# Forgetting attention and a feed-forward layer on one core: one more token group by seven half products, score tiles paired across batches, the last product but one in halves, and a new order

## The chip, the core and the metric

The kernel runs on one core of a Trainium2 chip. The engines of the core (TensorE or PE, VectorE or DVE, ScalarE or ACT, GpSimd or POOL, SyncE or SP) each run their own list of instructions in order and wait for one another by semaphores; PEld is TensorE's loading of weights. The metric is the device time of one execution in microseconds (us); lower is better. 359.41 us is the median of 3 runs of the kernel before (358.56 to 359.49).

## The reference

The inputs are q, k and v of 8 batches, 8 heads, 576 tokens and 64 dimensions, a forget gate f for each token of each head, and three weights with a vector of gains. Cut to what matters:

```python
scores = q @ k.T / sqrt(64)
cum    = cumsum(log(clip(f, 1e-4, 1)))             # along the tokens
scores = where(causal, scores + cum_i - cum_j, -1e9)
o      = softmax(scores) @ v                       # 8 batches, 8 heads, 576 x 64
x      = o as 4608 tokens x 512
xn     = x / sqrt(mean(x * x) + 1e-6) * rms_g
out    = (silu(xn @ w_gate) * (xn @ w_val)) @ w_out     # 512 -> 1536 -> 512
```

## The kernel before

Attention works by batch. Keys lie on the partitions and queries on the columns, in blocks of 128 tokens; the last block has 64. A *score tile* is the product of one block of keys with one block of queries for all 8 heads (128 x 1024, in PSUM), and for the last 64 queries one tile holds two blocks of keys. So a batch has 10 tiles in its four whole query blocks and 3 for its last one. Heads have only 64 dimensions, so TensorE holds the scores' matmuls (L525) in another tiling, two side by side of 64 rows each. One *score block* is the matmuls of up to two tiles in a row. ScalarE takes the exponential (L544), GpSimd masks the tiles on the diagonal (L552), TensorE multiplies with the scaled values (L573; the gates' decay is folded into these values, and an added column gives the denominators), and VectorE divides (L592, L596). ScalarE and GpSimd make the norm (L621, L626, L627, L635). q and k are turned by DMA (L435), for the first two batches on TensorE (L450, L456), and so are the normed tokens (L643 in the first batch).

The feed-forward layer works on 9 groups of 512 tokens: group g below 8 is the first 512 tokens of batch g, and group 8 gathers the last 64 tokens of all batches. Groups 0 to 6 go the plain way: for each of 12 blocks of 128 of the 1536 middle dimensions there is one product with w_gate and one with w_val, each of 4 matmuls with 512 columns (L830, *gates* in this text), a tanh on ScalarE (L842) and two VectorE operations (L844, L837). Groups 7 and 8 use `seven()` instead: the product is split into 2 x 2 halves and computed from 7 half products in place of 8, each 4 matmuls with 256 columns (L765). That needs differences of token halves (L754), sums of weight halves once (L732), copies on ScalarE (L782, L784, L787), additions on VectorE (L790, L792), silu on ScalarE (L800, L810), and the product of the two branches on VectorE (L806) or on GpSimd (L816). The table for silu is loaded behind the last exponential (L733), since exp and silu don't share one.

The output product of every group is by seven too (`project`): TensorE L905, sums of its left side L880 to L889, copies L912, additions L915, and stores L933 and L935 on the queues of SP and ScalarE. In the last group one product is computed in two halves, so that its first half is added and stored while the second is computed.

What sets the order: the program records *units* (a few instructions of one engine with what they need and which buffer slots they hold). A table ORDER gives each unit its place in one common list, and a table SLOTS gives each buffer its slot; every engine then runs its instructions in the order of that list. Nothing is decided while the kernel runs. All loads of q, k, w_gate (wg), w_val (wv) and of the first batches' v are issued by GpSimd (L332, L344, L355, L365), between its masks.

In the rows, `ff` and `late` are PSUM buffers of TensorE's products (`late` are the four that served the scores until those were over), `sc` the score tiles, `PT` the exponentials (later 32-bit buffers of group 7 and 8), `sm` the sums of the output product, `hT` the middle layer, `ores` the output.

Of the kernel before, what the change touches and what calls it, by code (L numbers as in the profile page):

```python
# [29 lines left out]
SEVEN = {7, 8}  # L30
# [9 lines left out]
    "iomEmFkzkAl5l6kgkhl0l1kQkRlKlLjRjSlylzkqkr0s0B0v0J0S0M0P0W0I0N0O0T0X0Y18141a1c1i1m1q1s1w1D11191b1d1r"  # L40
    "1B1J1F1P1Z1U241v1Q2q2M3u213g2T3q3w333r3z3E3G353F3L3R3Q3X4e4a4g4q4u4D4J5f4z4M4U535m5g5q4G4H58592R5x5V"
    "5L5W5Z624n4o4X4Y5U646f6U6r6F6J6d6e5G5H7c6v6k6l5n5o7p7a7g7l7j5S5T65666x7u7y807H7P7W878p7r7s6s6t7C8g8n"
    "8x8G8V8I8P7F7G7Y7Z7w919c969m9y9D6D6E85868w888u8v8l8maw9I9P9W9M8K8L9N9ObC9Va7ai9ZalauaCba9S9TasatbpbG"
    "bMbTc2c5cbciaTaUadae9dcjcCcpcwcAdcbNbOaAaBaDbfaIaJbrbsdkcOcUdecXc0c1cFcGd6d1d8dFdgdudBdPetcncodvdwel"
    "e0e5ebekepeweEcecfdDdEcqePfbeSfdfifmeiejeCeDdWfUereseXeYgmftfBfJfSfgfhfYfZgtg3g9gggugHgSgMgRgogpfQfR"
    "h2h0hdh5hthHhwhDhkhlgegfhshZiiiViMiOiThahbiaibijhmhShThJhKiuj7jljrjqjyjzi4i5kNjQjXkwk3kekBkkkoklkmjD"
    "jEiKkVl2lalflwlBlIjTjUiZj0lglYm1mpmbmlmqlulvl8l9lkjxlNlOk6k7n8mRmXn4n3mymzmfmgnwn7nnnsntnNnTnQnUlDlE"
    "lllmo0o2o5obojoFoxoEn1n2m8m9mLoLpwoSp2pkpo1517161h1g1n1t1x1I1L20232i2m2n2r3I3N3M4147494c4h4l544r4V5D"
    "5Q616b686g757t7I7L7U818q8y8D8J8H8R8Q8W959b9e9h9Q9Xa5aaafavaZb7bibnc4cacccgcDcWcMcVdndxdydIdJdOe4e7ec"
    "egeFeKeNeQeReWf1f4fXg8gcghgjgngYh7h3hehvhFhEi7iciqiyiGjbjkjKjWkZl4lblelnlqlQm2lVlZmcmjmsmwn5nenhnrnz"  # L50
    "nCnLnRnXoeo6oaoiomoQoUoVoXpHpT1j1u1A1E1G1C1H1O1T1Y2e2l2p2t2x2v2y2D2G2L8rbwcuf5f6464E4K5c5t5B575u5C5R"
    "6i6p6w6A6G6z6I6OdmfWhiktku8O90949o9r9s9f9i9j929l9p9v9z9A9B9G9Hjvldm7pqpraNbFbLbZcJcKcscxcycPd0d3d7da"
    "dbdddidjfEhLiHkXkYdZenexeGeLeMfufGfHeZf8fcfofrfsflfzfAh1jeooqlqmhChUhYipiviwimiIiJixj2j5jdjmjnjajfjg"
    "jAlsmioGoHlrlHlPmxn9nalTlWlXmdmCmIndninjmQmVmWnmpuq6q9qao7oholp0p6p7oqouovoPp4pbpspypzpepipjqkqpqFqL"
    "qM1K2u2c2o2A2k2z2s2w2F2E2X2J2N342O322W3138392Y373e4p3l3i3y1V2625272f222d282b2j363k3h3j3p3O403U454b3Z"
    "6a5s52675E5A6n3t3S3B3P3Y2K3a2S3d3m3f483o3s4f3n3x3v3A3H424i76704v7q6N7e5X6c63696j5K6C606o6W6V7d74797i"
    "7J8t838d8A6m6K6H6R716h6u6q6y6B7h827m7z8c6Z7k7b7f7o8z8M8F8N987x7X7K7V848b8k8j8o8s7n7D7v7E7ObYcmc3c6ct"
    "ahb6ayaFbcbkbAbqbubJa6aEajaqaMaVbob3bebx9YaragakazbbcdbtbXclbvbKbBbPbUbQcrchcvcBc9czckcEcIaHbdaSb0bj"
    "axaOaGaPaYfkfLfxfDfVdQfwdXeafIeueIeBeHeOdGeddLdTemfFfTfMg0g4e6eoeheqevdKdVdUdYe1eVf3f2fjfnfffpfqfvfy"
    "eyf7eJf0fehhhAhrhBhIfCg5fKfPgigkgwgsgvgEgDhcgIgNhjiUjuj1j6jCgqgTgPgUgZh6hGhnhxhNgOhqgXh4hugdgLglgrgQ"  # L60
    "hQi3hXi6i9iNjGjjjFjIhMhWhRhVi2ihj3iBiPjii8iridikizkpkGkxkMl7kakCkykDkIkOm6kWltmrjVlck0k4lhmNmUmTmYn0"
    "jLjZk9kdkfmvmGmHmKmPmJmZmOmSn6lJlSlRlUm5m0mhmamemmmkmBmAmDmMlilFlolClMp9phpgplppnJo9nMnSodofonokopos"
    "ozoYoKoRp5pcpxpnpvpDpmpCpBpEpGoWp3oZp1pdoTptp8pfpAoroJoCoIoMnAnGnEnFnOnVo3o1o4o8ocowotoyoDjYogq2q5no"
    "nIpaqOqopLpOqnqqpQpUpVq1qzpXq0qeqtqKqjqQqdqfqbqyqrqCqJqSqWqZqVr5qDqGqTrarlrZqXr3qxqPqEqNqYqUrbr2rkrn"
    "rhrBr0r4qHqRrcrfrjrirurCryrIr8rsrFrLrMrRrvrGr9rgrzrDrorrrArVrQs4s0sgrmrprKrXrwrErOs2sbsesaskrtrPslso"
    "snsqshsxrqrxrWrUrHrJrSs1rNrYs3s6s7sis8svs5sfs9scspstswsmsEsHsBsVrTssszt3sJsMt7tDsrsusjsDsAsysKsPt8te"
    "sZtksCsIsdsFsTsNsQsLt0t6sStbsOsWtEtMt4twtntrsYt1sRsUtdt5tit2tptstotRt9tctqtytmtttxtCtztLtGtVtgtIu6uf"
    "tHtJtBtN3T4L4m4w4F4Z4Q5r4d4C4I4R7M7N4W5b5a5p5l5F8S8T5P5Ybybz4N5M8h8i8E8Z939k9g9q9w9UbHbI9n9x979C8U9F"
    "iWiX9J9Ra2a39Ea4bVbWcLcZcQd5cHcNcTdtg6g7cYd2d9dhd4dliQiRdCdHezeAdfdqf9faigiLitjcilisiAiSk1k2iYj4jhjp"
    "jojwkbkcjHjMjOjPjBjJqAqBjNkjk8kUk5knkvkHmnmokikskLkPl3ljnfnglplAmtmulxlGm3m4nbnunlnyncnqnvnBoNoOnpnx"  # L70
    "nDnHnknKoAoBnPnWnYnZpFpZqgqhpIpWpKpPpJpNpSq3q7q8pMpRq4qcpYqsqvqwqIr1r6r7qiqurdretathtjtusGsXtftltXtY"
    "tvtAtKtPtFtQtTtUu3uauduetOtSu0u1tZu5u2uotWu4uiuuuyuzuwuxu7u9u8ucubuhumunujukuvuFuIuJuGuHugulurusupuq"
    "utuAuDuEuBuC")
SLOTS = (
    "751b7a63635242211938006514304071702032672611556343322a53745b716946107b411165046361283342572233750170"
    "0a332b5330447841512610233962121b43705800557a606704213b46125269710710236153322a65015453732879107b4233"
    "614622043701427063180553291b406753613a26323322117030156104312200101106701300145111032106711011001542"
    "0107301411062100141051054321010107337106210451501711125602301030110560142030171010506016310112116104"
    "2721075101044106310476310520102701410101410761034060125107141010600265113014347017501124310601047101"
    "0351106702710213510761004450153017207106100053241230322211203053242032210101205204321003250240301350"  # L80
    "3324310313333003042321242100533423213430110125234132003331231102103220331301123162514033620133073520"
    "2152530072000633350711217010601120070304153612111000011112310201132002010301002000101310123101110032"
    "0113113300030021101011000013010210121132000010100103311230132001110120102103201101012112001220100100"
    "3001220101011011131001013011221102113210030011310210121011000321110112310011030011310000132000211011"
    "1022012100131023000311021102010111310120001010132002311301013012000121110000110101003111273604415751"
    "0064236357211106007124230037561153541106247213030100164145037112102430232017414210001232312173021020"
    "3303411200212030401233152252100206104015420120240002231242112014133200174232107211773642720120003124"
    "3471656523470")
# [960 lines left out]
```

## Time and profile before

| | us |
|---|---|
| median of 3 runs | 359.41 |
| the profiled execution | 359.02 |
| its span (first to last instruction) | 357.2 |
| TensorE busy | 340.5 |
| VectorE, ScalarE, GpSimd busy | 277.1, 252.8, 194.6 |

The profiled execution is a run like the others; 1.8 us of its time lie outside the span. The granted clock of TensorE is 0.999 of full speed over the span. Busy times of the engines overlap, so they don't add up to the span; that of TensorE is 95% of it.

### The profile page before, as it was taken

To read this page: it belongs to the slowest core of one execution; us is meant where nothing else is said; L and a number is where in the kernel's file an instruction comes from. 1 tells how busy PE (TensorE), PEld (TensorE's weight loads), DVE (VectorE), ACT (ScalarE), POOL (GpSimd) and SP (SyncE) were. 2 spreads that over 40 slices of the span, in tenths; PEclk is the share of its full clock that TensorE was granted. 3 is DMA by queue.
4 is the path that set the end of the run, shared out by engine and by line. 5 is a ranking of instruction groups with operands and counts; after the bars stand their busy time and mean duration, and the time that the engine had idled before them with its cause. 6 is when DMAs were issued, how large, how long until landed. Compare 5 with 4: busy or idle time off the path is not lost.

```text
span 357.2 us, 10310 instructions
## 1 busy us (share of the span) xinstructions
PE 340.5 (95%) x4202; PEld 250.6 (70%) x4202; DVE 277.1 (78%) x507; ACT 252.8 (71%) x417; POOL 194.6 (54%) x241
## 2 busy tenths in 40 slices
...
GB/s 126 218 202 225 198 144 89 142 137 181 160 140 165 165 221 111 154 131 139 142 154 144 152 131 151 135 149 146 61 29 83 54 2 140 61 2 0 2 106 131
DMA packets 161510, 44.86 MB, mean 126 GB/s; under 512 B 147060, under 2 KB 160888, under 8 KB 161464
## 3 DMA queue, kind: packets, MB, share of 16 engines
...
q8 instruction: 33, 0.54, 0.6%
q10 hardware_dynamic: 592, 0.52, 0.4%
...
## 4 chain that ended last, share of the span: by engine, by line
PE 80%; DVE 6%; DMA 4%; POOL 3%; issue 3%; ACT 2%; SPq 0%; DVEq 0%; POOLq 0%; ACTq 0%
PE ff L830 37%; PE ff L905 16%; PE sc L525 7%; PE ff L573 6%; PE ff L765 4%; PE late L765 4%; PE late L905 3%; DMA qk<-in_q_dram 2%; POOL qk L332 2%; DMA QT<-qk 1%; PE ff L456 1%; ACT PT L544 1%; DVE KT L754 1%; DVE ga L844 1%; DVE hT L837 1%
## 5 line engine op out<-in xcount | busy, mean ns | idle before, releaser
L544 ACT ACTIVATE PT<-sc 128x1024 bf16<-128x1024 f32 x96 | 95.7, 1024 | 20.3 <-PE sc L525 20.1
L830 PE MATMUL ff<-xT,wv 128*128 128x512 bf16 (+2 forms) x528 | 85.0, 302 | 0.3 <-DVE x L596 0.2
L830 PE MATMUL ff<-xT,wg 128*128 128x512 bf16 (+2 forms) x528 | 84.4, 301 | 0.8 <-DVE ores L915 0.3
L842 ACT ACTIVATE th<-ff 128x512 f32<-128x512 f32 x84 | 49.4, 599 | 30.9 <-PE ff L830 26.1
L844 DVE SCALAR_TENSOR_TENSOR ga<-th,ff 128x512 f32<-128x512 f32 x84 | 57.1, 683 | 17.6 <-ACT th L842 16.0
L837 DVE SCALAR_TENSOR_TENSOR hT<-ga,ff 128x512 bf16<-128x512 f32 x84 | 57.0, 684 | 16.1 <-PE ff L830 14.6
L552 POOL TENSOR_SCALAR_AFFINE_SELECT PT<-PT 128x1024 bf16<-128x1024 bf16 x32 | 36.4, 1138 | 49.2 <-ACT PT L544 48.1
L830 PEld LDWEIGHTS <-wg 128*128 128x128 bf16 x528 | 42.2, 98 | 24.9 <-issue 1.2
L830 PEld LDWEIGHTS <-wv 128*128 128x128 bf16 x528 | 41.5, 98 | 24.3 <-issue 0.7
L905 PEld LDWEIGHTS <-hT 128*128 128x128 bf16 x432 | 41.5, 98 | 6.5
L573 PEld LDWEIGHTS <-PT 128*128 128x128 bf16 (+1 forms) x896 | 32.7, 103 | 10.8 <-issue 1.9
L573 PE MATMUL ff<-Vs,PT 128*128 128x65 bf16 (+1 forms) x896 | 37.7, 196 | 0.4 <-POOL PT L552 0.4
L525 PE MATMUL sc<-QT,KT 64*128 64x128 bf16 (+1 forms) x960 | 34.5, 214 | 2.4 <-ACT KT L468 0.9
L915 DVE TENSOR_TENSOR ores<-ores,ff 128x512 f32<-128x512 f32 (+1 forms) x39 | 26.2, 671 | 13.0 <-PE ff L905 11.2
L596 DVE TENSOR_TENSOR x<-ff,rden 128x256 f32<-128x256 f32 (+1 forms) x80 | 33.9, 424 | 3.0 <-ACT xn L635 0.3
L525 PEld LDWEIGHTS <-KT 64*128 64x128 bf16 x960 | 24.9, 97 | 16.0 <-issue 12.7
L485 POOL TENSOR_TENSOR Vs<-v,decT 128x512 bf16<-128x512 f32 (+1 forms) x30 | 33.2, 1114 | 5.0 <-DMA v<-in_v_dram 4.9
L905 PE MATMUL ff<-wo,hT 128*128 128x256 bf16 x288 | 35.4, 273 | 0.0
L905 PEld LDWEIGHTS <-sm 128*128 128x128 bf16 x324 | 30.7, 98 | 5.2 <-DVE sm L886 0.9
L626 POOL TENSOR_SCALAR ms<-sq 128x2 f32<-128x2 f32 (+2 forms) x26 | 6.7, 260 | 50.5 <-ACT junk L621 48.8
L332 POOL DMA_DIRECT2D qk<-in_q_dram x36 | 31.2, 873 | 1.1 <-POOLq L1033 0.8
L332 POOL DMA_DIRECT2D qk<-in_k_dram x36 | 31.5, 880 | 0.4 <-issue 0.3
...
## 6 DMA issues: line engine op xcount, KB each, us to landing
...
qk<-in_q_dram POOLq DMA_DIRECT2D x28, 128.0 KB, 5.2
qk<-in_k_dram POOLq DMA_DIRECT2D x28, 128.0 KB, 5.5
...
wg<-in_moe_w_gate_dram POOLq DMA_DIRECT2D x3, 512.0 KB, 10.0
wv<-in_moe_w_val_dram POOLq DMA_DIRECT2D x3, 512.0 KB, 11.2
...
```

Of the source, the lines that this page charges most:

```text
L332: nc.gpsimd.dma_start(out=T_qk[h.slot][0:n, :].rearrange("p (h d) -> p h d", d=D), in_=src[b, :, p0:p0 + n, :].rearrange("h p d -> p h d"))
L485: eng.tensor_tensor(T_Vs[hv.slot][0:n, j, :, 0:D], T_v32[h.slot][0:n, :, :], bcast(dj, D), ALU.mult)
L525: nc.tensor.matmul(t[:, par, c:c + n], lhsT=kt[r, p, kj * 128:(kj + 1) * 128], rhs=qt[r, p, qi * 128:qi * 128 + n], start=not x, stop=True ...
L544: nc.scalar.activation(T_of_p[hp.slot][:, 0:2 * half].rearrange("p (a c) -> p a c", a=2)[:, :, 0:cols], T_sc[h.slot][:, :, 0:cols], ACT.Ex ...
L552: nc.gpsimd.affine_select(out=d, in_=d, pattern=[[0, 8], [1, n]], compare_op=ALU.is_ge, fill=0.0, base=0, channel_multiplier=-1)
L573: nc.tensor.matmul(T_ff[hpo.slot][r0:r0 + n, p * 65:p * 65 + 65], lhsT=T_of_p[h.slot][:, c:c + n], rhs=vs[:, kj, 2 * p + par, :], start=(k ...
L596: nc.vector.tensor_tensor(d, po[r0:r0 + n, :, 0:D], bcast(r[r0:r0 + n, :], D), ALU.mult)
L830: nc.tensor.matmul(T_ff[h.slot][:, c:c + n], lhsT=w[:, dc, fc * 128:(fc + 1) * 128], rhs=xT[:, dc, t0:t0 + n], start=(dc == 0), stop=(dc = ...
L837: nc.vector.scalar_tensor_tensor(hT, in0=three[0], scalar=0.5, in1=three[1], op0=ALU.mult, op1=ALU.mult)
L842: th = act(0.6, key - 0.1, lambda: nc.scalar.activation(T_th[ht.slot], T_ff[hg.slot], ACT.Tanh, scale=0.5), [ug], take=[ht])
L844: a = dve(0.69, key - 0.1, lambda: nc.vector.scalar_tensor_tensor(T_ga[ha.slot], in0=T_th[ht.slot], scalar=1.0, in1=T_ff[hg.slot], op0=ALU ...
L905: nc.tensor.matmul(t[:, s * HD:(s + 1) * HD], lhsT=a()[:, fc, s * 128:(s + 1) * 128], rhs=w[:, fc, :], start=(not more and s == ss[0] and ...
```

## The change

1. Group 6 is computed by seven half products too. The buffers for the differences of tokens were one for each of the two groups; now there are two slots which the three groups take in turn.
2. Each batch has 13 score tiles, an odd number. Before, the last tile of a batch was a block by itself. Now it makes a block with the first tile of the next batch, and 53 blocks take the place of 57.
3. In the last group a second output product (with `w22`, the half A of the output) is computed in two halves, each added and stored by itself; the buffers hold for the added stores.
4. ORDER and SLOTS are other tables.

```diff
-SEVEN = {7, 8}
+ACROSS = True
+SEVEN = {6, 7, 8}
...
 ORDER = (
-    "0302000104050h0j0k0A0w0l0o0g0i0C0p0z0a0b0F0Z1006070c0d08090e0f0m0n0t0u0x0y0q0r0D0E0K0L0Q0R1k1l0U0V12"
+    "03020001050604070H0v0t0s0y0i0j0m0n0u0c0d0z1C0D0g0h0e0f0a0b0k0l08090A0B0L0M0o0p0P0Q13141G1H26271f1g2m"
...
-                 sc=2, ff=4, hw=8, sw=8)
+                 sc=2, ff=4, hw=8, sw=8, xs=2)
...
-            if len(todo) == 2 or (b == 0 and kjs[-1] == qi) or kjs[-1] == LAST:
+            if len(todo) == 2 or (b == 0 and kjs[-1] == qi and qi < LAST) or kjs[-1] == LAST and (not ACROSS or b + 1 == B):
                 score_block(todo, qkey(b, qi, i))
                 todo = []
...
-        hs = spare[g - G]
+        hs = Hold("xs", 4 + 3 * 2 * 4)
...
-            return t[hs.slot].rearrange("p c t -> p (c t)")[:, 1536 + (i % 2) * 512:2048 + (i % 2) * 512].rearrange(
+            return t[spare[hs.slot].slot].rearrange("p c t -> p (c t)")[:, 1536 + (i % 2) * 512:2048 + (i % 2) * 512].rearrange(
...
-                       ready + ([X[need]] if need else []) + [Lsum["g", 1], Lsum["v", 1]], take=[hs], give=[hx])
+                       ready + ([X[need]] if need else []) + [Lsum["g", 1], Lsum["v", 1]], take=[hs], give=[hx, hs])
...
-            return pe(0.435, key, emit, deps, take=list(take), give=list(give) + [hx])
+            return pe(0.435, key, emit, deps, take=list(take), give=list(give) + [hx] + ([hs] if k in X else []))
...
-        o = [Hold("ores", 1 if g < B else 2 + 2 * (halved and i == 1)) for i in range(4)]
+        o = [Hold("ores", 1 if g < B else 2 + 2 * (halved and i < 2)) for i in range(4)]
...
-        m3 = product(lambda: T_sm[h4.slot], w22, f4, [m5, v4, u4], give=[h4], more=True)
-        store(A, 0, 1, plus(f4, A, A, [m3, v3], give=[f4]))
+        if not halved:
+            m3 = product(lambda: T_sm[h4.slot], w22, f4, [m5, v4, u4], give=[h4], more=True)
+            store(A, 0, 1, plus(f4, A, A, [m3, v3], give=[f4]))
         if halved:
-            f5.n = 2
+            f4.n = f5.n = 2
+            for s in range(2):
+                m3 = product(lambda: T_sm[h4.slot], w22, f4, [m5, v4, u4], give=[h4] if s else [], more=True, ss=(s,))
+                store(A, 0, 1, plus(f4, A, A, [m3, v3], c=slice(s * HD, (s + 1) * HD), give=[f4]), s)
```

Line numbers behind the diff's first lines are one higher in the changed kernel (L365 becomes L366, L552 becomes L553, and so on).

How the order moves is shown at three places. The first is GpSimd's queue while the kernel starts, before the change: loads of v, wg (w_gate) and wv (w_val) between the first masks (`AFFINE_SELECT`).

```order
L355 DMA v_69<-in_v_dram 128x8x64
L365 DMA wg<-in_moe_w_gate_dram 128x4x512 x2
L552 AFFINE_SELECT PT_82<-PT_82 128x1024
L365 DMA wv<-in_moe_w_val_dram 128x4x512
L552 AFFINE_SELECT PT_81<-PT_81 128x1024
L344 DMA wt<-in_k_dram 128x8x128
L365 DMA wv<-in_moe_w_val_dram 128x4x512
L365 DMA wg<-in_moe_w_gate_dram 128x4x512
```

The same queue after the change, from its third mask on (ms and rs are the norm's two small steps).

```order
L553 AFFINE_SELECT PT_77<-PT_77 128x1024
L356 DMA v_71<-in_v_dram 128x8x64
L627 TENSOR_SCALAR ms<-sq 128x1
L628 TENSOR_TENSOR rs<-ms,mhalf 128x1
L553 AFFINE_SELECT PT_82<-PT_82 128x1024
L366 DMA wv<-in_moe_w_val_dram 128x4x512
L627 TENSOR_SCALAR ms<-sq 128x1
L628 TENSOR_TENSOR rs<-ms,mhalf 128x1
L553 AFFINE_SELECT PT_80<-PT_80 128x1024
L366 DMA wv<-in_moe_w_val_dram 128x4x512
L356 DMA v_70<-in_v_dram 128x8x64
```

The first load of w_val stood behind the first mask, and stands behind the fourth now; the loads of w_gate and of w_val stood next to each other, and now further loads of q, k and v stand ahead of them. On TensorE's list the first gate with w_val stands behind 80 score matmuls, 64 transposes of q and k, 48 value matmuls and 8 transposes of normed tokens before the change, and behind 128, 96, 88 and 12 after it; the 48 matmuls with w_gate ahead of it are as many as before.

The second place is ScalarE's list where the exponentials end, after the change: `th` under L843 is a tanh of the plain way, L734 the load of the silu table, L785, L783 and L788 the copies of group 6, L801 its silu.

```order
L545 ACTIVATE P_83<-sc_120 128x512
L843 ACTIVATE th_101<-ff_112 128x512
L734 ACT_TABLE_LOAD
L734 ACTIVATE junk<-rgT 1x1
L785 COPY PT_80<-late_4563 128x512
L636 ACTIVATE xn_91<-x_85,rs 128x512
L783 COPY ff_112<-late_4562 128x512
L843 ACTIVATE th_100<-ff_113 128x512
L801 ACTIVATE th_101<-late_4562 128x512
L783 COPY late_4562<-late_4560 128x512
```

Before the change the list goes on at this place with norms, tanh and the copies of group 7.

```order
L544 ACTIVATE P_83<-sc_119 128x512
L842 ACTIVATE th_101<-ff_115 128x512
L635 ACTIVATE xn_91<-x_89,rs 128x512
L544 ACTIVATE PT_81<-sc_120 128x1024
L842 ACTIVATE th_100<-ff_113 128x512
L912 COPY ores_108<-ff_113 128x512
L782 COPY ff_115<-late_4897 128x512
L787 COPY PT_79<-ff_115 128x512
L784 COPY PT_75<-late_4896 128x512
```

The copies of the first group by seven stood behind the last exponential with a tanh and an output copy between, and now come right behind the last of the exponentials, with tanh of the plain way still among them.

The third place is the end of ScalarE's list, copies (L912) and stores of the last group (L933 stores a half, L935 a whole piece), before the change.

```order
L912 COPY ores_104<-ff_112 128x512
L800 ACTIVATE th_101<-ff_113 128x512
L935 DMA out_dram<-ores_105 64x2x256
L933 DMA out_dram<-ores_108 64x256
L912 COPY ores_107<-ff_112 128x512
L935 DMA out_dram<-ores_107 64x2x256
L933 DMA out_dram<-ores_108 64x256
L935 DMA out_dram<-ores_104 64x2x256
```

The same end after the change.

```order
L913 COPY ores_104<-late_4563 128x512
L913 COPY ores_108<-ff_112 128x512
L936 DMA out_dram<-ores_105 64x2x256
L934 DMA out_dram<-ores_106 64x256
L913 COPY ores_104<-ff_112 128x512
L936 DMA out_dram<-ores_104 64x2x256
L934 DMA out_dram<-ores_108 64x256
L934 DMA out_dram<-ores_106 64x256
L934 DMA out_dram<-ores_108 64x256
```

The list ended with the store of a whole piece (ores_104) behind the last addition; it ends with halves of two pieces now (ores_106 and ores_108), and VectorE's last addition, a whole piece into ores_104 before, is the second half into ores_106.

## Rows read from the trace of the kernel before

**Rows 1.** The page's busy line: us, share of the span, instructions.

```profile
PE 340.5 (95%) x4202; PEld 250.6 (70%) x4202; DVE 277.1 (78%) x507; ACT 252.8 (71%) x417; POOL 194.6 (54%) x241
```

**Rows 2.** Stretches: us, busy PE, PEld, DVE, ACT, POOL, then PEclk, DMA, GB/s.

```profile
20.00:40.00 20.00, 19.71 (x380) 18.66 (x377) 17.67 (x34) 14.87 (x24) 14.33 (x20) 1.00 1.35 210
60.00:80.00 20.00, 18.94 (x340) 16.31 (x339) 14.93 (x28) 19.15 (x32) 14.07 (x19) 1.00 1.70 138
```

**Rows 3.** The chain that ended last, two pieces: start, us, what.

```profile
241.88 4.32 PE ff L830 x20
...
304.52 2.18 PE ff L765 x20
```

**Rows 4.** Groups by line: count, busy us, mean ns, idle before.

```profile
L842 ACT ACTIVATE th<-ff 128x512 f32<-128x512 f32 x84 | 49.4, 599 | 30.9 <-PE ff L830 26.1 <-DVE hT L837 2.4 <-ACT ores L912 0.8
...
L816 POOL TENSOR_TENSOR hT<-PT,PT 128x512 bf16<-128x512 f32 x12 | 15.9, 1348 | 26.1 <-ACT PT L810 14.6 <-DVE PT L790 6.4 <-ACT PT L784 5.1
...
L784 ACT COPY PT<-late 128x512 f32<-128x512 f32 x7 | 4.0, 585 | 0.3 <-PE late L765 0.3
...
L754 DVE TENSOR_TENSOR QT<-xT,QT 128x512 bf16<-128x512 bf16 x1 | 0.4, 424 | 0.0
```

**Rows 5.** Timeline, groups by seven: start, us, engine, line, operation.

```profile
313.18 2.69 POOL L816 TENSOR_TENSOR hT<-PT,PT 128x512 bf16<-128x512 f32 x2 [0.56 <-ACT PT L810]
...
314.65 1.50 DVE L754 TENSOR_TENSOR KT<-xTr,QT 128x512 bf16<-128x512 bf16 x1
...
317.89 0.60 PE L765 MATMUL late<-KT,wg 128*128 128x256 bf16 x4
...
318.59 0.60 PE L765 MATMUL late<-QT,QT 128*128 128x256 bf16 x4
```

**Rows 6.** The same view, TensorE around a score block.

```profile
123.47 1.03 PE L830 MATMUL ff<-xT,wv 128*128 128x512 bf16 x4
124.43 0.62 PE L525 MATMUL sc<-QT,KT 64*128 64x128 bf16 x16
124.98 1.04 PE L830 MATMUL ff<-xT,wv 128*128 128x512 bf16 x4
```

**Rows 7.** TensorE up to its first gate with w_val.

```profile
24.04 0.40 PE L643 MATMUL ff<-ident,xn 128*128 128x128 bf16 x4
24.27 1.06 PE L830 MATMUL ff<-xT,wg 128*128 128x128 bf16 x16
25.17 0.53 PE L573 MATMUL ff<-Vs,PT 128*128 128x65 bf16 x12
25.54 1.05 PE L830 MATMUL ff<-xT,wg 128*128 128x128 bf16 x16
26.43 2.04 PE L830 MATMUL ff<-xT,wv 128*128 128x128 bf16 x32
```

**Rows 8.** GpSimd's queue: third w_gate load, issue behind the fourth mask.

```profile
17.36 0.77 POOL L365 DMA_DIRECT2D wg<-in_moe_w_gate_dram  x1
...
26.74 0.92 POOL L355 DMA_DIRECT2D v<-in_v_dram  x1
```

**Rows 9.** DMA issues at three times: KB each, us to landing.

```profile
qk<-in_k_dram POOLq DMA_DIRECT2D x1, 128.0 KB, 4.6
...
wg<-in_moe_w_gate_dram POOLq DMA_DIRECT2D x1, 512.0 KB, 13.7
...
wv<-in_moe_w_val_dram POOLq DMA_DIRECT2D x1, 512.0 KB, 11.7
```

**Rows 10.** The groups by line, scores of 128 columns.

```profile
L525 PE MATMUL sc<-QT,KT 64*128 64x128 bf16 x640 | 27.0, 226 | 2.4 <-ACT KT L468 0.9 <-ACT PT L544 0.7 <-DMA QT<-qk 0.7
```

**Rows 11.** The timeline at the end, additions and the last store's issue.

```profile
350.83 0.42 DVE L915 TENSOR_TENSOR ores<-ores,ff 128x256 f32<-128x256 f32 x1 [0.54 <-PE ff L905]
...
352.14 0.69 DVE L915 TENSOR_TENSOR ores<-ores,late 128x512 f32<-128x512 f32 x1 [0.89 <-PE late L905]
...
352.86 0.64 ACTq L935 DMA_DIRECT2D out_dram<-ores  x1
```

More of the change, by code (lines that the diff above doesn't have):

```diff
@@ L40 @@
[L40 to L73, printed above, removed]
-SLOTS = (
[L75 to L88, printed above, removed]
@@ new lines @@
+    "hjk2k3kgkhkQkRlUlVkIkJkBkCk8k9lblcmhmim6m70G0K0C0I0Y0R0V110N0S0J0O1l1012171k1x1e1o1m1q1w1L1i1n1t1A1N"
+    "1B1I1M1Q1Y1T201j1r181d2k0X2J242a2i2j21252d2g3t2q2x2W2D2K332O361J2b0W0Z433a3u3h3F3R3L3Q3i3j4h4i4H474k"
+    "4x48494K4L5e4Q50545f5r5V5I5L5t5u5l5m6b6e4T4U5M5N6Y686r6x6f5E5F6o6p7O6H6Z746T777f7u7A6K6L7d7e7U7F7K7Q"
+    "7Y8784887p7q8m8n958f8O8t6v6w8d8e8D5R94999f9h9n8y8z7D7E9F9o9B9w9M7w7x9x9yb59Wa2aa9r9s9S9TbvajapauataF"
+    "aMaJakalaPaQcpb3bibqbdbJbObZc3azaAaKaL9Ubnb9bab1b2cEcgcvcAcqbLbMaWaXcMcDcJd1cOd2dbd5dwc9cacZd0dcdsdE"
@@ new lines @@
+    "dLdQeje6endldmdHdIeLeueWeGe1e2eqereIeffufyfAfzg0eQeRf0f1gdfOfVfYgVfhfifmfnfWgigIgldOdPgmgnfbgOgTh5gX"
+    "h8hbhmggghgtguhvhBhRi0hMi9idiliqhwhxhkhliBhdh6h7gbgcgMiwiSiViMiaibhEhFkxiXj2jijfjpjAjGkmjljmjWjXj0jO"
+    "jYjTktkFkzl0kdkejPjQjqkTl2l8kukvkkkljbjolnlqlwlxlEjJjKiNiOl4lHlPlWmalklllNlOmrmcmfmom0m1lsltmlmAmKmQ"
+    "mImRn0mYmwmxmMmNnln5ncnhn8nmnqnCnG151c16191s1F1E1K1S1W1V1Z292p2l2s2C2H2N2Q383e3f3m3D3N3S4a4s4w4z4C5n"
+    "5w656n707576797l7v7B7L8286898b8k8x8G8R9l9q9C9H9L9R9Za4aCaSbobubybDbGbKbQbVcycKcLcRd4dadodtdJdRdZe5e8"
@@ new lines @@
+    "edeyeHeSeVfLfTgAgHh1h9hahhhzhVhHhNi1i4ieikinitiTiYjDjIjNjRk6kbkfkjkLkUkVl3lolvlzlLm5mdmemjmsmymCmHmP"
+    "mSn7nbnjnnnxnBnKnZohop1h1p1D1X281R1U222e2h232c2o2v2y2X31373g3o9GcugagKgL3b3r3M3X4r4t424O4R5a4X5p5x5Q"
+    "5W5O63679ma5bteaeb8q8l8u8F8M8N8Y92938C8W909d9i9j969b9clFm4nvokol9VaUaZbRbXbYb8chcic2c8cecBcGcHcncrcs"
+    "dYfKg3lBlCdye4e7etezeAf5f9faepf2f6fsfwfxfffIfJmvnwqcqZr0hGihimjwjBjCisiyiziFiCiRiWjdjeiZj3j4kckqmbos"
+    "otk1knkNl6l9lakSkXkYlKlTlYmmmpmqmzmFmGphq0q6rarbngmWnrp9pepfnQocodnzoboionpvpwoJpnpooCoGpPqSqT2w2P2I"
@@ new lines @@
+    "2T2Y344j3B3G4o2E2Z2V32353U4c4b4l4q444G4D5256625D662f3s2r2B3C3J3Z3P3Y4g2U3n30393y3x3O3E3K3T4f4I4V4n6C"
+    "4p6m6d4F4S4M4W514J5b4P555j4v4B4A4E4N4m4Z4u4y596P6u7r695s7i737b5g6c5o5P6j5v6A5A5G6I717h787c7m8a8s8h8r"
+    "8E7G8p7X838A6t6X6J6U727a7n7o7s7z6q7t6z6Q7R8B8Z8L8T9a8K9891979k7y7P7C7H7Z7S858c8g8oc0ctcccfcxa3aca7ab"
+    "ahcmcwczcCcIaYbsb6bmbHbebwbpbxbBagaTamayb0bNbUbWc1c4avb7aRb4bfcFcUcXd3d7cbcNcjcocYbCc5bIbPcda6bjafai"
+    "bri3ici7i8iiecfdeDfgfkfpgefHfMgjdedBdgdndKflfUfqftfZdveidUe0esf7fvfefrfCeOfjeTeZfoeoeEexeFeKe3f3eeek"
```

37 lines of the change are left out of this document (33 added, 4 removed).

## The prediction

> **What bounds the kernel now.** I read the busy line of the page first, then the table by stretch of time, then the chain that ended last. The reader is to see in the first that TensorE is busy 340.5 us of the 357.2 us span [rows 1], and in the second that from 20 us on it has hardly a gap: 19.71 and 18.94 us busy in two stretches of 20, the second being among the worst [rows 2]. So behind the first 25 us the kernel lasts as long as its list of matmuls, and an edit is worth what it takes out of that list, plus or minus the gaps that it opens or shuts. In the chain the reader is to see what a matmul of either width costs when it runs without a gap [rows 3]. The gaps lie at the start (before 26 us TensorE waits for loads and for the exps), in single waits in the middle, and behind the last matmul. I take these places one by one.
>
> **Group 6 by seven.** Taken out: 24 products of 4 matmuls with 512 columns. 20 such matmuls take 4.32 us [rows 3], so 4 take 0.864, and the 24 take 20.74 us. Put in: 2 x 3 units x 7 = 42 half products of 4 matmuls with 256 columns. 20 take 2.18 us [rows 3], so 4 take 0.436, and the 42 take 18.31. TensorE gains 2.43 us. This stands only if nothing else becomes late, since the other engines get work: ScalarE gives up 12 tanh of 599 ns and gets 18 copies and 12 silu at about 585 ns, the duration of such a copy [rows 4]; that is 17.6 for 7.2, so +10.4 us. GpSimd gets 6 products of 1348 ns, +8.1 us [rows 4]. VectorE gives up 24 operations and gets 22, none longer, so it has no more to do. ScalarE's and GpSimd's additions lie beside TensorE's 18 us of group 6, and both were idle a quarter of the span or more [rows 1]; I cost them at nothing while that cover lasts, and come to where it may fail.
>
> One place shows what happens when it fails. While GpSimd ran two of its products (313.18, 2.69 us), a difference of tokens on VectorE took 1.50 us [rows 5] where one takes 424 ns [rows 4], and a few products later a TensorE group that begins at 317.89 had its successor begin only at 318.59, 0.70 later, where 4 matmuls take 0.436: 0.26 us lost [rows 3, 5]. Group 6 brings one more such set of differences and 6 more products on GpSimd. One hit of the same size is +0.26, and I take +0.3; the bounds are 0 and 2.4 (rival 2). The Trainium skill ("SBUF — State Buffer", section "🔬 SBUF: two separate sides") says why this may be: VectorE and GpSimd share one pair of ports, taken for a whole instruction, and a VectorE operation that reads two operands from SBUF or runs in a fast mode stands still meanwhile. The 1.50 us agrees with that. By the rule alone the six products more could hold VectorE up for 8.1 us, and the sum, were TensorE to wait for all of that, would be some 365; the row shows 0.26 at one place.
>
> **Score tiles paired across batches.** A block of scores runs on TensorE in another tiling. A gate of 4 matmuls begins at 123.47 and the scores behind it at 124.43, 0.96 later instead of 0.864: about 0.10 for going over. The 16 matmuls of the block take until 124.98, 0.55 us [rows 6]; at 0.864 us for 2048 columns, 128 columns need 0.054, and two matmuls run beside each other in this tiling, so 8 x 0.054 = 0.43 would do: 0.12 lost inside each block. The blocks go from 57 to 53, the changes into that tiling from 57 to 54 (in one place two blocks follow one another). 4 x 0.12 + 3 x 0.10 = 0.78 us gained. Bounds: 0.5 (nothing for going over) and 1.0.
>
> **The start.** This is where the new order speaks against the change. In the kernel before the first gate that reads w_val begins at 26.43 [rows 7]. Ahead of the same gate the new order puts 48 more score matmuls (3 blocks of 0.55 [rows 6], 1.65), 36 more transposes (0.23 for 4, 24.04 to 24.27, is 2.07), and 40 more value matmuls (0.37 for 12, 25.17 to 25.54, is 1.23): 5.0 us, more than which only its waits can add [rows 7]. Wanted from about 31.4 on, then, if the waits up to there are as long as before. When does the weight come? Its load now stands on GpSimd's queue behind the mask of the fourth query block's second pair, and GpSimd was through with that mask at 26.74 [rows 8]. Two bounds. From below: counted in the KB that the profile gives for each load, the loads on this queue up to and with the first w_val are 8 x 128 + 4 x 256 + 5 x 256 + 3 x 512 = 4864 KB, just what stood up to and with the third w_gate load in the order before, which landed 13.7 us after its issue at 17.36, at 31.0 [rows 8, 9]. From above: another w_val load took 11.7 us from the end of such a backlog [rows 9], which from 26.74 would be 38.4. Between them: a load of 128 KB near the program's start took 4.6 us [rows 9]; 384 KB more at the 210 GB/s of this stretch [rows 2] are 1.9, so 6.4 us by itself with little ahead, and 26.74 + 6.4 = 33.1. I take that, as little is still under way in front of it by then: +1.7 us, with the ends at -0.4 and +7.0. The exps point the same way: TensorE's gate stands behind three more blocks of scores, and they want ScalarE's exps of the blocks ahead.
>
> **The middle.** The first scores of batch 2 waited 0.7 us for a transposed q [rows 10], and the whole stretch 60 to 80 lost 1.06 [rows 2]. The new order brings both this batch's loads and its scores forward. I take half of the wait as gone, -0.4, with -0.7 and +0.7 as bounds.
>
> **The end.** The last VectorE addition was a 512-column one, 0.69 us; now it is a half, 0.42, so -0.27 [rows 11]. But on ScalarE's queue two stores now stand behind the last addition, where one stood, and an issue there takes 0.64 [rows 11]: +0.37 together. I take +0.3; the bounds are -0.3 (the other queue takes the last piece) and +0.4.
>
> **Sum.** The profiled execution took 359.02 us, 0.39 below the median of the runs shown, and I work from it: 359.02 - 2.43 - 0.78 + 1.7 - 0.4 + 0.3 + 0.3 = 357.7. I forecast 357.6 us, 0.5% under the median. A measurement of this kernel tells about 0.3% from no change: faster is below 358.3, slower above 360.5.
>
> **Rivals.** 1. The start costs nothing, since the backlog has moved on by the time of the issue and the weight lands at 31.0, and the wait of batch 2 goes too: 359.02 - 2.43 - 0.78 - 0.7 + 0.3 = 355.4. For it speaks that the KB ahead come out even; against it, that the queue's issue waits for a mask. Chance 0.17.
>
> 2. The seven products of group 6 give back their gain: ScalarE, GpSimd and VectorE can't drain the half products while the last exps and norms still run, and TensorE's buffers come free late. The place above lost 0.26; nine such losses over 42 half products return the 2.43: 360.0. For it speaks that the stretch from 300 to 320, which has group 7 in it, held such a place with fewer exps around; against it, that even there TensorE stood still so seldom. The Trainium skill's rule on the shared ports, named above, would act in just this way. Chance 0.15.
>
> 3. Slower: the load of w_val is late by the upper bound. TensorE runs its list in order, so all stands behind that gate: 38.4 - 31.4 = 7.0 in place of 1.7 gives 362.9. It decides from a wait of 4.6 us on, a landing at 36.0 (357.6 + 2.9 = 360.5). For it speaks that the w loads of the kernel before took 11.7 and 13.7 us in the backlog [rows 9] and this one is issued late; against it, that the order has fewer weights in front of it than before. Chance 0.21.
>
> My forecast has the rest, 0.47, with its own range 356.2 to 359.0. The range for all: from 354.6, under rival 1 by what the middle may still give, to 361.5, which takes in rival 2 and the nearer part of rival 3 and leaves its far part, about one in eight, out. Faster: 0.17 and four fifths of 0.47, 0.56 with a little of rival 2; same: the rest of the forecast and most of rival 2, 0.21; slower: 0.23.
>
> **What would show it.** TensorE's busy time should fall by about 3 us, to 337.3, with the clock as it is. The first matmul with w_val should begin near 33, waiting for its load; at 31.5 rival 1 holds, behind 36 rival 3. The group-6 half products should follow one another at 0.44; if they start 0.7 apart again and again, with the idle time ended by ScalarE's copies or VectorE's sums, it is rival 2. Score blocks should still cost 0.55 each, just fewer of them. The prediction is wrong in its core if TensorE's busy time does not fall, or if the idle time before 30 us changes by more than 5.

## The result and the profile after

The changed kernel takes 363.54 us (median of 4 runs, 362.97 to 365.0) where the kernel before took 359.45 (358.56 to 359.87): a ratio of 1.0109, interval 1.0075 to 1.0144. It is slower by about 4 us, above the range that the prediction gave. The profiled execution took 363.75 us with a span of 362.0, 4.8 more than before.

The page of the changed kernel, its busy line, answers to [rows 1].

```profile
PE 333.9 (92%) x4247; PEld 256.8 (71%) x4274; DVE 280.0 (77%) x506; ACT 263.6 (73%) x435; POOL 204.4 (56%) x247
```

TensorE has less to do, as forecast, and waits more. (27 matmul records are missing here: 4274 weights were loaded for 4247 matmuls, so 333.9 is too low. The experiment e6 below, whose list of matmuls is the same and whose records are whole, has 335.9, which is 4.6 under the kernel before.) The prices of the list held. These are pieces of the chain that ended last: a stretch of half products of the groups by seven, and one score block, with start, us, what, and the number of matmuls; they answer to [rows 3, 6].

```profile
173.85 0.55 PE sc L526 x16
...
278.79 1.31 PE ff L766 x12
```

A half product costs 1.31 / 3 = 0.437, and in group 6 they follow one another at that pace; a score block costs 0.55. So the loss lies in waits, and in two places. The first is the start. TensorE's first matmul in the kernel before and in the changed one (start, us, engine, line, operation, and in brackets the idle time before it and what ended it), and below it the stretch up to the first gate with w_val in each (us, then busy us of PE, PEld, DVE, ACT, POOL, then the granted clock, DMA share and GB/s):

```profile
5.69 0.61 PE L450 MATMUL ff<-ident,qk 128*128 128x128 bf16 x4 [5.69 <-DMA qk<-in_q_dram]
...
7.88 0.76 PE L309 MATMUL ff<-ident_f,hT 64*128 64x64 f32 x5 [7.88 <-ACT hT L300]
```

```profile
0.00:26.43 26.43, 17.25 (x254) 13.89 (x255) 17.99 (x46) 16.42 (x19) 24.08 (x36) 1.00 1.35 182
...
0.00:33.76 33.76, 19.92 (x378) 16.22 (x378) 25.41 (x61) 25.20 (x32) 31.94 (x46) 1.00 1.39 173
```

TensorE was idle for 9.2 us ahead of that gate before, and is for 13.8 now. Of these 4.7 us more, 2.2 come from the first matmul, which now needs a result of ScalarE from the forget gate in place of a q. But the matmuls ahead of the gate take only 2.7 us more, not 5.0: four transposes took 0.61 us as late as 21.11 in the kernel before and 0.40 from 11.98 on in the changed one. Together that is 7.3 us, near the 1.7 and 5.0 of the forecast. TensorE's timeline goes on:

```profile
33.76 1.07 PE L831 MATMUL ff<-xT,wv 128*128 128x128 bf16 x16 [0.87 <-DMA wv<-in_moe_w_val_dram]
...
47.88 0.64 PE L526 MATMUL sc<-QT,KT 64*128 64x64 bf16 x32 [1.34 <-DMA QT<-qk]
56.53 0.52 PE L526 MATMUL sc<-QT,KT 64*128 64x64 bf16 x24 [0.22 <-DMA KT<-qk]
```

The first gate with w_val begins at 33.76 (it was 26.43 [rows 7]), and waits 0.87 us for its load. Two more waits follow that the prediction did not name: the scores of the last 64 queries of the first two batches wait for transposed q and k. The chain shows how these hang together:

```profile
38.35 9.29 DMA qk<-in_q_dram
...
47.66 1.84 SPq L436
...
49.55 6.93 DMA KT<-qk
...
56.53 0.52 PE sc L526 x24
```

A k that is wanted at 56.5 was turned from 49.55 on, though its load had landed at 42.6: on SP's queue it stood behind the turn of a q whose load landed at 47.6.

The second place is larger. Timeline of VectorE, GpSimd and TensorE from 202 us on, all operations of the three that matter:

```profile
202.48 0.77 POOL L333 DMA_DIRECT2D qk<-in_q_dram  x1
...
202.96 4.38 DVE L884 TENSOR_TENSOR hT<-hT 128x1536 bf16<-128x1536 bf16 x1
...
203.28 1.06 POOL L486 TENSOR_TENSOR Vs<-v,decT 128x512 bf16<-128x512 f32 x1
...
204.28 1.09 POOL L553 TENSOR_SCALAR_AFFINE_SELECT PT<-PT 128x1024 bf16<-128x1024 bf16 x1
...
205.32 0.36 POOL L493 CAST Vs<-decT 128x40 bf16<-128x40 f32 x1
205.49 1.03 POOL L486 TENSOR_TENSOR Vs<-v,decT 64x512 bf16<-64x512 f32 x1
...
207.27 0.67 DVE L838 SCALAR_TENSOR_TENSOR hT<-ga,ff 128x512 bf16<-128x512 f32 x1
...
208.00 1.02 PE L831 MATMUL ff<-xT,wg 128*128 128x512 bf16 x4 [1.67 <-DVE hT L838]
...
210.33 1.44 PE L831 MATMUL ff<-xT,wv 128*128 128x512 bf16 x3 [1.19 <-DVE hT L838]
```

A sum on VectorE (one of the four that each output product needs) took 4.38 us. The same instruction takes 0.95 elsewhere. Beside it GpSimd runs four operations with no gap between them, and the sum ends 0.8 us after the last of them, as if it had stood still for 3.4 us and then run. (Its row begins 0.3 us ahead of the first of the four, beside the issue of a load.) Behind it on VectorE's list stood the operation (L838) that frees a buffer of TensorE, which then waited 1.67 and, with the next one, 1.19 us. The table by stretch adds a third loss: busy us of PE, PEld, DVE, ACT, POOL, then the granted clock, DMA share and GB/s.

```profile
200.00:210.00 10.00, 7.42 (x108) 4.71 (x107) 8.67 (x9) 8.46 (x13) 9.36 (x11) 0.99 1.05 121
210.00:220.00 10.00, 9.39 (x83) 6.34 (x85) 7.27 (x16) 3.77 (x8) 1.31 (x3) 0.84 1.35 169
```

After the two gaps the granted clock of the next ten microseconds is 0.84, so part of it ran at 1.2 GHz: the three matmuls at 210.33 take 1.44 together, where three took 0.81 in other places. VectorE runs 48 operations of the sum's form. Added up they take 10.5 us more than 48 times 0.95, where it was 3.7 in the kernel before, whose longest took 1.63. Of the others that were held TensorE waited behind three: at 161.01 (1.81 us), at 307.14 in group 6 (1.72 us), and here:

```profile
224.44 2.47 DVE L881 TENSOR_TENSOR sm<-hT 128x1536 bf16<-128x1536 bf16 x1
...
224.90 1.10 POOL L553 TENSOR_SCALAR_AFFINE_SELECT PT<-PT 128x1024 bf16<-128x1024 bf16 x1
...
225.96 1.84 POOL L486 TENSOR_TENSOR Vs<-v,decT 128x512 bf16<-128x512 f32 x1
```

Here it goes both ways: the sum ends 0.9 us after the mask, which is through at 226.0, and GpSimd's product beside it takes 1.84 us in place of 1.05, so that now it is the one that stands.

The end answers to [rows 11]:

```profile
356.93 2.14 ACTq L934 DMA_DIRECT2D out_dram<-ores  x3
...
357.01 0.41 DVE L916 TENSOR_TENSOR ores<-ores,late 128x256 f32<-128x256 f32 x1
```

The last addition is a half, 0.41 us, and three stores follow each other on ScalarE's queue. From the start of the last addition to the end of the span it is 5.0 us (362.0 - 357.01), against 5.1 before (357.2 - 352.14): the half saves 0.3 and the stores behind one another cost about as much.

### The profile page after: what moved, and what is told of

It is laid out like the page before. It is cut to its first block, busy times and chain, and to the rows that moved or that the text cites. A ratio compares the mean times of both kernels' runs of the same rounds, so it can differ in the third digit from the quotient of the medians.

```text
span 362.0 us, 10449 instructions
## 1 busy us (share of the span) xinstructions
PE 333.9 (92%) x4247; PEld 256.8 (71%) x4274; DVE 280.0 (77%) x506; ACT 263.6 (73%) x435; POOL 204.4 (56%) x247
## 4 chain that ended last, share of the span: by engine, by line
PE 73%; DVE 13%; DMA 5%; issue 4%; ACT 2%; POOL 1%; SPq 1%; DVEq 0%; ACTq 0%
PE ff L831 26%; PE ff L906 19%; PE ff L766 6%; PE late L766 6%; PE ff L574 6%; PE sc L526 5%; DMA qk<-in_q_dram 3%; PE late L906 2%; DMA KT<-qk 2%; DVE hT L838 1%; DVE ga L845 1%; DVE x L597 1%; DVE sm L881 1%; DVE sm L890 1%; DMA hT<-in_f_dram 1%
## 5 line engine op out<-in xcount | busy, mean ns | idle before, releaser
L831 PE MATMUL ff<-xT,wg 128*128 128x128 bf16 (+2 forms) x468 | 72.3, 292 | 2.9 <-DVE hT L838 1.7
L831 PE MATMUL ff<-xT,wv 128*128 128x128 bf16 (+2 forms) x465 | 71.8, 293 | 3.1 <-DVE hT L838 1.6
L838 DVE SCALAR_TENSOR_TENSOR hT<-ga,ff 128x512 bf16<-128x512 f32 x72 | 48.7, 682 | 17.5 <-PE ff L831 16.7
L843 ACT ACTIVATE th<-ff 128x512 f32<-128x512 f32 x72 | 42.8, 597 | 22.9 <-PE ff L831 19.7
L845 DVE SCALAR_TENSOR_TENSOR ga<-th,ff 128x512 f32<-128x512 f32 x72 | 48.8, 682 | 7.7 <-ACT th L843 6.1
L831 PEld LDWEIGHTS <-wg 128*128 128x128 bf16 x480 | 37.6, 98 | 21.5 <-issue 2.4
L831 PEld LDWEIGHTS <-wv 128*128 128x128 bf16 x480 | 37.4, 98 | 21.6 <-issue 2.4
L817 POOL TENSOR_TENSOR hT<-PT,PT 128x512 bf16<-128x512 f32 x18 | 25.2, 1416 | 47.9 <-ACT PT L811 18.5
L553 POOL TENSOR_SCALAR_AFFINE_SELECT PT<-PT 128x1024 bf16<-128x1024 bf16 x32 | 36.6, 1144 | 23.8 <-ACT PT L545 23.5
L916 DVE TENSOR_TENSOR ores<-ores,ff 128x512 f32<-128x512 f32 (+1 forms) x41 | 27.4, 671 | 15.5 <-PE ff L906 14.2
L526 PE MATMUL sc<-QT,KT 64*128 64x128 bf16 (+1 forms) x960 | 32.2, 209 | 3.5 <-DMA QT<-qk 1.3
```

Of the source, the lines that this page charges most:

```text
L526: nc.tensor.matmul(t[:, par, c:c + n], lhsT=kt[r, p, kj * 128:(kj + 1) * 128], rhs=qt[r, p, qi * 128:qi * 128 + n], start=not x, stop=True ...
L553: nc.gpsimd.affine_select(out=d, in_=d, pattern=[[0, 8], [1, n]], compare_op=ALU.is_ge, fill=0.0, base=0, channel_multiplier=-1)
L831: nc.tensor.matmul(T_ff[h.slot][:, c:c + n], lhsT=w[:, dc, fc * 128:(fc + 1) * 128], rhs=xT[:, dc, t0:t0 + n], start=(dc == 0), stop=(dc = ...
L838: nc.vector.scalar_tensor_tensor(hT, in0=three[0], scalar=0.5, in1=three[1], op0=ALU.mult, op1=ALU.mult)
L843: th = act(0.6, key - 0.1, lambda: nc.scalar.activation(T_th[ht.slot], T_ff[hg.slot], ACT.Tanh, scale=0.5), [ug], take=[ht])
L845: a = dve(0.69, key - 0.1, lambda: nc.vector.scalar_tensor_tensor(T_ga[ha.slot], in0=T_th[ht.slot], scalar=1.0, in1=T_ff[hg.slot], op0=ALU ...
```

## The experiments

My theory after the result: two causes, apart from each other. First, sums on VectorE stand still while GpSimd goes on without a gap, and the new order put them there; second, the start's queues (the order of the first 20 us was left as it is). The rivals: the sum is only where TensorE's wait shows; or the start alone decides; or any shift of GpSimd's list would do. The kernels are the changed one with small edits. An edit of the order takes a unit by its place in the common list and puts it behind another one:

```diff
+        place = list(order)
+        for a, b in MOVES:
+            order.remove(place[a])
+            order.insert(order.index(place[b]) + 1, place[a])
```

**One wait more, and its control.** Unit 1187 is the sum that took 4.38 us. Behind it GpSimd gets a copy of 128 x 8 numbers. In the run e1 it reads the sum's result, so GpSimd has to wait for the sum; in the control e0 it reads a constant.

```diff
+PROBES = {1187: 1187}
...
                 u.emit()
+            if u.rank in PROBES:
+                nc.gpsimd.tensor_copy(probe, tap[PROBES[u.rank]]()[:, 0, 0:8])    # e0: decT[:, 0, 0:8]
```

> Control for the next run. The changed kernel with one tiny GpSimd copy (128 x 8) between two of its instructions at the place where VectorE's sum of 0.95 us took 4.38 us; the copy reads a constant and waits for nothing. Port theory (the sum stands still because GpSimd has the shared port and its next instructions follow without a gap): a copy without a wait leaves GpSimd's chain as dense as it was, the sum stays above 3 us, time 363.5 within 0.7. Rival (any shift of GpSimd's instructions changes the encounter by luck): the sum falls below 2 us and the time falls by 3 or more.

> The changed kernel with one wait more: the same copy, but it reads the result of VectorE's sum, so GpSimd can't begin its next product before that sum is through. Port theory: the sum takes 0.95 to 2 us in place of 4.38, TensorE's gaps of 1.7 and 1.2 us behind it go, and the clock stays up, so 3 to 5 us less than the changed kernel: 358.5 to 360.5. Rival 1 (the sum is only where the wait shows, TensorE would wait there for another thing): 363 to 364. Rival 2 (the wait added makes GpSimd's masks late): slower than the changed kernel, 364 to 366.

Measured: e0 1.0101 (1.0066 to 1.0136), e1 1.0054 (1.0026 to 1.0083). The intervals overlap, but the two ran side by side: even without the two longest of e0's 12 times the means of their times are 1.8 us apart (95% interval 0.9 to 2.8, worked out from the single times). The traces agree. The control first: the sum takes 4.51 us, and GpSimd's copy changed nothing. (In e3 and e7 below, which leave this place as it is, the sum takes 4.4 as well.)

```profile
205.66 4.51 DVE L889 TENSOR_TENSOR hT<-hT 128x1536 bf16<-128x1536 bf16 x1
...
205.95 0.20 POOL L1030 CAST probe<-decT 128x8 bf16<-128x8 f32 x1
...
206.10 1.05 POOL L491 TENSOR_TENSOR Vs<-v,decT 128x512 bf16<-128x512 f32 x1
```

With the wait, in e1:

```profile
205.90 0.95 DVE L889 TENSOR_TENSOR hT<-hT 128x1536 bf16<-128x1536 bf16 x1
...
206.93 0.18 POOL L1030 COPY probe<-hT 128x8 bf16<-128x8 bf16 x1 [0.74 <-DVE hT L889]
...
207.08 1.03 POOL L491 TENSOR_TENSOR Vs<-v,decT 128x512 bf16<-128x512 f32 x1
207.37 1.57 DVE L892 TENSOR_TENSOR sm<-sm,hT 128x1536 bf16<-128x1536 bf16 x1
208.08 1.80 POOL L558 TENSOR_SCALAR_AFFINE_SELECT PT<-PT 128x1024 bf16<-128x1024 bf16 x1
```

GpSimd waits 0.74 us, the sum takes 0.95, and the kernel is about 1.7 us (0.0047 of 359.8) faster than the control. A wait added made the kernel faster. The theory had expected 3 to 5 us under the changed kernel, and it is 2.0 by the ratios: part of the pressure moved on, since the next sum then took 1.57 and the mask beside it 1.80 in place of 1.09. The table of the stretch from 200 to 240 us shows the gain, in the kernel before, e0, e1 and the next run, e2:

```profile
200.00:240.00 40.00, 40.00 (x450) 27.09 (x449) 29.55 (x54) 25.24 (x43) 19.91 (x28) 1.00 1.08 142
...
200.00:240.00 40.00, 35.90 (x408) 23.66 (x408) 31.00 (x50) 25.72 (x43) 23.60 (x29) 0.91 0.92 126
...
200.00:240.00 40.00, 37.90 (x494) 25.62 (x490) 33.29 (x55) 30.06 (x52) 26.71 (x34) 1.00 1.11 141
...
200.00:240.00 40.00, 39.01 (x514) 26.72 (x512) 32.62 (x60) 31.32 (x53) 27.29 (x36) 1.00 1.18 142
```

TensorE was never idle there before, and for 4.1, 2.1 and 1.0 us in the three runs.

**Three waits.** Also at 161 (with GpSimd's product put behind the wait) and at 224.

```diff
+MOVES = ((941, 942),)
+PROBES = {942: 942, 1187: 1187, 1292: 1286}
```

> The changed kernel with such waits at the three places where such a sum was held longest in the middle of the program (at 161, 203 and 224 us; at the first of them GpSimd's product is moved behind the wait). Port theory: some 1.5 us less than with the one wait, 357 to 359.5. Rival (only the long one matters, since the others are hidden by TensorE's work queued ahead): the same as with the one wait within 0.5.

Measured: 0.9988 (0.9955 to 1.0021), 359.44 us: 0.012, some 4.4 us, under the changed kernel, and level with the kernel before. Under e1 it is some 2.4 us, where 1.5 was expected. The rival (only the long one matters) falls. These two waits have no control of their own with a copy that doesn't wait.

**The neighbours moved, no wait.** The two products and the small copy beside the sum go further down on GpSimd's list.

```diff
+MOVES = ((1204, 1240), (1189, 1204), (1202, 1189))
```

> The changed kernel with no wait added, but the two GpSimd products and the small copy that followed each other during the sum at 203 us moved behind that queue's next load of q. Port theory: the sum stands still only as long as GpSimd goes on without a gap, so it takes 1 to 2.6 us in place of 4.38 and the time falls by 1.5 to 4 us, a ratio of 1.000 to 1.007. Rival (it was the wait added, or the later masks, that helped in the run with one wait): the sum stays near 4 and the ratio at 1.010.

Measured: 1.0073 (1.0043 to 1.0103). That is just above the theory's range, and the interval overlaps the changed kernel's, so the time shows no gain for certain. The timeline says why:

```profile
202.53 0.95 DVE L889 TENSOR_TENSOR hT<-hT 128x1536 bf16<-128x1536 bf16 x1
...
205.17 3.02 DVE L735 TENSOR_TENSOR KT<-QT,wv 128x1536 bf16<-128x1536 bf16 x1
...
205.31 2.05 POOL L491 TENSOR_TENSOR Vs<-v,decT 64x512 bf16<-64x512 f32 x2
...
207.30 1.10 POOL L498 CAST Vs<-decT 128x40 bf16<-128x40 f32 x1
```

Freed of its neighbours, the sum takes 0.95, so the rival (it stays near 4) falls. The chain that was moved meets another sum, of weights (L735), and now that one takes 3.02: it ends 0.8 us after the two products, and the small copy behind them, 0.36 before, takes 1.10. The stall goes where the chain goes: this is the strongest evidence for the mechanism.

**The start.** e3 issues the first w_val load two masks earlier on GpSimd's queue and puts the first scores of the last 64 queries three gates later; e7 changes only SP's queue, so that the k turn stands ahead of the q turn.

```diff
+MOVES = ((130, 104), (255, 270), (268, 255))     # e3
+MOVES = ((265, 255),)                            # e7
```

> The changed kernel with the start mended and nothing else: the first load of w_val issued before the third mask rather than behind the fourth, and the first scores of batch 0's last 64 queries three gates later on TensorE. In the changed kernel's trace TensorE waited 0.87 us for that load and 1.34 for those queries. Theory (the loads decide the start): 1.5 to 2.2 us less than the changed kernel, 361.3 to 362.0. Rival (the next late thing takes over, ScalarE's exps or VectorE's chain): within 0.7 of 363.5.

> The changed kernel with SP's two turns in the other order and nothing else: the start by itself. If the start and the held sums are two separate causes that add, 1 to 2.6 us less than the changed kernel, a ratio of 1.003 to 1.008. If the start doesn't count, 1.011.

Measured: e3 1.0106 (1.0042 to 1.0171), no gain, as its rival had it; e7 1.003 (1.0003 to 1.0057), by the ratios 2.8 us less than the changed kernel, at the far end of what was expected. In e3 both waits that it was meant to take away are gone, and this row took their place on TensorE:

```profile
58.22 0.82 PE L531 MATMUL sc<-QT,KT 64*128 64x64 bf16 x24 [2.88 <-DMA KT<-qk]
```

So these waits stand in a row and the last of them, SP's, decides: mending the earlier ones only made the last one longer. The table of waits of the three-waits run e2 has the same entry (engine, line waited for: us in total, times, longest):

```profile
PE sc L536 <- DMA KT<-qk: 2.6, 1, 2.6
```

**Both together.** e5 is the three waits and the turn; e6 has e3's edits too.

> The kernel with the three waits, and on SP's queue the turn of k of batch 0's last 64 tokens ahead of the turn of q of batch 1's, in place of behind it. In the three-waits run TensorE waited 2.61 us for that k at 57.8: its load had landed at 41.4, but SP stood with the q turn ahead of it, whose load landed at 47.1. Start theory (one queue's order holds TensorE up): that wait goes, 2 to 2.6 us less than with the waits alone, a ratio of 0.993 to 0.996 against the kernel before. Rival (another turn or an exp takes its place): within 0.7 us of the waits alone, a ratio of 0.998 to 1.000.

> The same, and the start's two other edits with it: the first w_val load before the third mask, and the first scores of batch 0's last 64 queries three gates later. If the three are waits in a row, each seen only when the one behind it is gone, another 0.5 to 1.5 us less than without these two, a ratio of 0.989 to 0.994. Rival: no difference from the run without them, since ScalarE's exps and GpSimd's masks set the pace of the first 30 us.

Measured: e5 357.22 us, 0.9927 (0.9897 to 0.9958); e6 356.55 us, 0.989 (0.9854 to 0.9927). Both beat the kernel before. The turn was worth 0.006, some 2.2 us, as expected; whether e3's edits add to it is not settled, as the intervals overlap. SP's queue in e5 shows the turn of k (the second row) done at the time of its load, 43, in place of 49.5:

```profile
39.55 1.28 SPq L446 DMA_TRANSPOSE QT<-qk  x1
42.87 1.17 SPq L446 DMA_TRANSPOSE KT<-qk  x1
47.98 1.17 SPq L446 DMA_TRANSPOSE QT<-qk  x1
```

**A fourth wait.** At the sum of group 6's output among GpSimd's new products.

```diff
-PROBES = {942: 942, 1187: 1187, 1292: 1286}
+PROBES = {942: 942, 1187: 1187, 1292: 1286, 1717: 1717}     # and units 1714, 1719 behind 1717
```

> The fastest kernel so far (three waits, turn, start) with one wait more, at the sum of group 6's output at 301 us, which took 1.72 us in place of 0.95 beside two of GpSimd's products and left TensorE waiting 0.69 us for an addition queued behind it; the two products go behind the sum. Port theory: that wait goes, 0.4 to 0.8 us less, a ratio of 0.985 to 0.989. Rival (GpSimd's products are then late themselves and hold up the sums of the next group): the same or up to 1 us more, 0.989 to 0.992.

Measured: 356.46 us, 0.9901 (0.9884 to 0.9919), not to be told from e6: the rival's range, not the theory's. The sum fell from 1.72 to 0.95 us, and TensorE's wait behind it from 0.69 to 0.27, so 0.4 us may be there; but the next difference of tokens, which now meets the products, took 1.25 where it had taken 0.89:

```profile
300.16 0.95 DVE L900 TENSOR_TENSOR sm<-hT,sm 128x1536 bf16<-128x1536 bf16 x1
...
301.33 5.15 POOL L827 TENSOR_TENSOR hT<-PT,PT 128x512 bf16<-128x512 f32 x4
301.63 1.25 DVE L765 TENSOR_TENSOR QT<-xTr 128x512 bf16<-128x512 bf16 x1
```

## Why the prediction was wrong

*TensorE's list, -2.43 and -0.78.* Right: the unit prices are those of the rows, and with the two causes taken away the kernel stands 3.2 us under the kernel before (359.77 to 356.55). Busy time fell by 4.6 us in the whole record of e6; where the 1.4 beyond the list come from stays open.

*"Shared port", +0.3 with the bounds 0 and 2.4.* This is the step that failed. The mechanism was seen, in a row of the trace and in the rule of the Trainium skill, and the price was taken from the one place where it had cost 0.26. Waits at three places gave back 0.012, some 4.4 us. Two things were missed. The place: I looked at group 6 and its six new products on GpSimd, where the term was not far off (TensorE waits 0.7 us behind the sum at 307.14). But the long stall lay in the stretch of attention, on sums that the change does not touch; only the new order had put them beside a run of scaling and masking on GpSimd. And the size: in the rows I read, a held operation stood beside one or two of GpSimd's, so it lost about one operation, and I took that for the price of any meeting. It can go on through several operations without a gap: four at 203 us, two in e8. It need not: in e1 the next sum stood for one product, and then the mask behind that product stood for the sum. What decides which of the two goes on is not shown. The Trainium skill ("SBUF — State Buffer", section "🔬 SBUF: two separate sides") says that whoever takes the shared pair of ports first has it for a whole instruction and the other stands still, for a VectorE operation with two operands in SBUF against one of GpSimd that reads SBUF. The traces agree that one stands while the other runs (4.38 us against 0.95, and 1.84 against 1.05 the other way round); that a run of instructions can win several times one after the other is what the 4.38 adds, and there the sum's row begins ahead of all four. The runs show that the sum is held beside these GpSimd operations (4.38 and 4.51 us) and not without them (0.95); that it is held at the ports, no run shows.

*The start, +1.7 between -0.4 and +7.0.* The gate with w_val was forecast at 33.1 and came at 33.76. That is near by luck. The landing, taken between two bounds, was well met; but the term counted on waits up to there "as long as before" and 5.0 us more of matmuls. The idle time was 4.7 us longer, only 0.87 of it for the load, and the matmuls took 2.7 more. (The end at -0.4 could not be had: the gate before waited for nothing, so a load that lands early gains nothing.) Wrong was the stretch behind it, which the sum put at nothing: SP's queue, which the prediction went past, held the k of the last 64 tokens behind a q. Turning these two round gave 2.2 to 2.8 us. With the 4.1 by which the ports' term was short that makes 6.3 to 6.9, against 5.9 between the forecast and the measured time. Rival 3 gave 362.9, near the measured time, but its mechanism (the load 7 us late) is not what happened.

*The middle, -0.4, and the end, +0.3.* The wait of 0.7 us for batch 2's scores has gone from the list of waits, and the end is as long as before, -0.1: both inside their bounds.

*Rival 2, 360.0 by late draining of group 6, the shared ports included.* The ports were the larger cause, but at another place and at nearly twice the price, and group 6's half products were not drained late; I gave it 0.15. The cover under which I cost ScalarE's 10 us and GpSimd's 8 us more at nothing did hold: in e9 and e6 they are still there, and both are faster than the kernel before.

What stays open: how much of the 4.4 us is TensorE's lower clock behind the gaps and how much the gaps. In the changed kernel's profile the clock costs some 1.3 us, an estimate from TensorE's busy time at the granted clock (1.45 us at 0.50 from 210 to 212, 2.00 at 0.71 from 212 to 214); in e7's, with the same gaps, nothing. Open, too, is whether e3's edits are worth anything next to the turn, and what the start up to the first gate could still give: no run changed its first matmuls, and in e6 TensorE is still idle for 12.55 of the first 26 us, where it was for 9.18 before.
